# Nine expert blocks chosen early instead of six, and high-word products first

## The chip, the cores and the metric

The kernel runs on one core of one Trainium2 chip. The metric is the device time of one execution in microseconds (us). Three runs of the kernel before gave a median of 1722.14 us (1718.45 to 1723.65).

## The reference

Attention with 32 packed keys per head feeds a dense layer pair, and its 4608 rows `x` of 512 numbers feed a mixture of eight experts:

```python
logits = x @ w_gate                                     # 8 experts
noisy = logits + log1p(exp(x @ w_noise)) * noise
top2 = the two largest of noisy, weights by softmax
for e in range(8): for k in range(2):                   # w1: 512x1024, w2: 1024x512
    out[mask] += weight * (relu(x[mask] @ w1[e]) @ w2[e])
```

Each token goes to two experts, so there are 9216 rows of expert work. Routing the drawn inputs with the reference gives 1138, 1148, 1197, 1127, 1082, 1133, 1212 and 1179 rows for experts 0 to 7. In blocks of 128 rows, the last of each expert padded, that is 75 blocks. Of the first 3456 tokens alone (six of eight batches), the counts are 833, 831, 898, 841, 829, 871, 895 and 914.

## The kernel before, in words

Three phases follow each other. Phase A is the packed attention, phase B the dense layers and the routing of tokens in steps of a batch (`todo`, `at(t, f)`: function f is issued in step t), phase C the expert blocks.

A block is 128 tokens of one expert. Its rows are fetched by four indirect transfers of POOL (`gather`, L978), transposed on DVE and split into a high word `xh` (copied on ACT) and a rest `xl` (subtracted on DVE) (`tx`, L991). `g1` (L1127) multiplies them by the first weights: two halves of 12 matmuls (xh by the high weights, xh by the low, xl by the high), 24 in all, and DVE transposes each half out of PSUM into a tile `h` of which there is one buffer. `tha` (L1149) applies relu in 16 small instructions, shared between ACT and DVE, into a tile `ht` of one buffer, and ACT copies the high word `hh`; `thb` (L1167) subtracts it on DVE to give the rest `hl`. `g2` (L1171) is 24 matmuls with the second weights, ACT scales the result by the gate (y) and POOL adds it to the output by an indirect transfer (store). Weights lie in two slots, each with a first and a second part of 4 MB; SP loads them (`wdma`, L910; `wload`, L1105), and a load is left out when the slot already holds the expert.

To have work while the last tokens are routed, six blocks of one expert with at least 768 rows are chosen from the first six batches (`early_count`, `early_rows`, L884 to L903), in step 214 of phase B. They use slot 0. In `run` (L1198) their PE, SP, DVE and ACT instructions are issued in an order written by hand, and in the same stretch the last tokens are routed (`L.logits`, `route`, `L.rank`, `L.slots`), their places scattered to a table, the remaining blocks planned (`main_rows`, L1003, on DVE), the table read back (`main_table`, `main_tr`), and the gather indices of the main blocks made (`main_sel`, `main_idx`). POOL's transfers wait in a list `queue`; `tick` (L1120) takes one off after each sixth matmul. After the early blocks comes the loop over the main blocks (L1297), in which the order on DVE, ACT and POOL is left to the planner, while PE and SP keep the written order: g1 of block k, then g2 of block k-1. In the early part too, PE runs g1 one block ahead or more: g1(0), g1(1), g2(0), g1(2), g2(1) and so on. The main blocks come alternately from the end of the list of experts and from its start, in slots 1 and 0. With up to 79 blocks in all, 75 are executed always, and those beyond only if they exist (`more`, L1318).

Of the kernel before, what the change touches and what calls it, by code (L numbers as in the profile page):

```python
# [10 lines left out]
F32 = mybir.dt.float32  # L11
FR = mybir.dt.float32r
I32 = mybir.dt.int32
BF = mybir.dt.bfloat16
# [7 lines left out]
P = 128  # L22
# [323 lines left out]
NBLK = 79  # L346
NEARLY = 6
NM = NBLK - NEARLY
# [509 lines left out]
class PhaseC:  # L858
# [16 lines left out]
    def counts(self, name):  # L875
        K, V, mp = self.K, self.K.nc.vector, self.mp
        mb = mp.tile([96, E], BF, name=f"mb{name}")
        V.tensor_copy(mb, K.msum)
        cps = K.pm.tile([P, 512], F32, tag="m", name=f"cps{name}")
        K.nc.tensor.matmul(cps[:, :E], K.ones, mb, start=True, stop=True)  # L880
        return cps


    def early_count(self):  # L884
        K, V, mp = self.K, self.K.nc.vector, self.mp
        self.cps = self.counts("e")

    def early_rows(self):
# [8 lines left out]
        re = mp.tile([NEARLY, 1], F32, name="re")  # L897
        K.nc.gpsimd.iota(re, pattern=[[0, 1]], base=0, channel_multiplier=1, allow_small_or_imprecise_dtypes=True)
        V.scalar_tensor_tensor(re, self.est[:NEARLY], 36.0, re, op0=ALU.mult, op1=ALU.add)
        self.rie = mp.tile([NEARLY, 1], I32, name="rie")  # L900
        V.tensor_copy(self.rie, re)
# [52 lines left out]
    def early_table(self):  # L954
        self.tbe = self.table(self.rie, NEARLY, "e")

    def early_tr(self):
        self.tpse = self.tr(self.tbe, NEARLY, "e")

    def early_tok(self):  # L960
        self.idxe, self.tok4e, self.gatee = self.tok(self.tpse, NEARLY, "e")

    def early_sel(self):
        self.gpse = self.sel(self.tok4e, NEARLY, "e")

    def early_idx(self):
        self.gidxe = self.gidx(self.gpse, NEARLY, "e")


    def slot(self, j):  # L970
        return 0 if j < NEARLY else (j - NEARLY + 1) % 2

    def at(self, j):
        if j < NEARLY:
            return 0, j, self.idxe, self.gidxe, self.gatee
        return self.slot(j), j - NEARLY, self.idx, self.gidxm, self.gate

    def gather(self, k, j=None, pace=None):  # L978
# [5 lines left out]
        rows = (K.x1d[:6 * S] if k < NEARLY else K.x1d).rearrange("n (q y) -> (n q) y", q=4)  # L984
# [18 lines left out]
    def main_rows(self):  # L1003
# [50 lines left out]
        ec, bs, kk = (mp.tile([NM, 1], F32, name=n) for n in ("ec", "bs", "kk"))  # L1054
# [24 lines left out]
    def consts(self):  # L1079
# [21 lines left out]

        self.planr = halves(1, NM, [[1, NM]], 0, "r")
        self.planc = halves(NM, 1, [[0, 1]], 1, "c")

    def wload(self, j, m, hs=(0, 1), after=()):  # L1105
        k = j - NEARLY
# [20 lines left out]
    def g1(self, k, between=None):  # L1127
# [5 lines left out]
        for fc in range(2):  # L1133
            p = self.ph.tile([P, 512], F32, tag="ph", name=f"ph{k}_{fc}")
            n = 0
            for d in range(4):
                for xx, ws in ((xh, 0), (xh, 1), (xl, 0)):
                    self.tick(K.nc.tensor.matmul(p, xx[:, d * P:(d + 1) * P], w[:, fc, ws, d, :], start=(n == 0), stop=(n == 11)))  # L1138
                    n += 1
# [31 lines left out]
    def g2(self, k, between=None):  # L1171
# [6 lines left out]
        for f in range(8):  # L1178
            for xx, ws in ((hh, 0), (hh, 1), (hl, 0)):
                self.tick(K.nc.tensor.matmul(p, xx[:, f * P:(f + 1) * P], w[:, f // 4, ws, f % 4, :], start=(n == 0), stop=(n == 23)))  # L1180
                n += 1
            if f == 3 and between:
                between()
# [14 lines left out]
    def run(self, L):  # L1198
        K, tc = self.K, self.K.tc
        with ExitStack() as ctx:  # L1200
# [15 lines left out]
            M0 = NEARLY  # L1216
# [13 lines left out]

            q += scatters(L.scatter[0]) + gather(4)
# [5 lines left out]
            def half():  # L1237
                route(4)
                self.thb(0)
# [20 lines left out]
            L.store()  # L1260
            self.tha(2, 0)
            rows = self.main_rows()
            next(rows)
            self.g2(1)
# [5 lines left out]
            next(rows, 0)  # L1270
            self.tx(5)
            while q:
                q.pop(0)(self.last)
# [11 lines left out]
            q[:0] = gather(M0 + 1)  # L1285
# [3 lines left out]
            self.g2(4)  # L1289
            self.tx(M0)  # L1290
            self.thb(5)
            while q:
                q.pop(0)(self.last)
# [3 lines left out]
            for k in range(M0, NSURE + 1):  # L1297
# [11 lines left out]
                if k + 1 < NSURE:  # L1309
                    self.wload(k + 1, 1)  # L1310
# [3 lines left out]
            total = K.nc.values_load(self.tmi, min_val=NSURE - 3 - NEARLY, max_val=NM)  # L1314
# [3 lines left out]
    def more(self, j, total):  # L1318
        if j >= NBLK:
            return  # L1320
        with self.K.tc.If(total > j - NEARLY):
# [81 lines left out]
```

## Time and profile before

| what | us |
|---|---|
| three runs | 1722.14 (median), 1718.45, 1723.65 |
| profiled execution, span | 1721.9 |
| PE busy | 1625.7 (94%) |
| DVE, ACT, POOL busy | 1132.5 (66%), 865.1 (50%), 565.5 (33%) |
| first matmul of block 0, g1 of block 9, last result copied | 852.47, 976.33, 1707.97 |

The page gives no other time for the profiled execution than its span. PE holds a matmul for longer than the next one needs to start, so its busy time is read here only for where it is broken. The two levels of its clock are 1.2 and 2.4 GHz; "granted" 1.00 is 2.4 GHz.

### The profile page before, as it was taken

The page shows a single profiled execution, that of the slowest core. Times are in us where ns is not written, and L with a number is a line of the kernel's source. Part 1 is how long each engine was busy: PE and PEld are TensorE (multiplying, and loading weights), DVE is VectorE, ACT ScalarE, POOL GpSimd, SP SyncE. Part 2 cuts the span into 40 slices and gives each one's busy share as a digit, 9 for nine tenths or more (in the row PEclk, how much of TensorE's full clock was granted, in tenths as well). Part 3 has the DMA queues.
Part 4 walks back from the last instruction along what each step waited for, and adds up shares of the span by engine and source line. Part 5 has one row for each costly group of instructions (what it writes and reads, how often), then busy time and mean ns, then how long its engine had stood idle before and what let it go on. Part 6 is the DMA issues. An engine that isn't in the chain of part 4 may idle for free.

```text
span 1721.9 us, 29366 instructions
## 1 busy us (share of the span) xinstructions
PE 1625.7 (94%) x10031; PEld 1378.8 (80%) x10031; DVE 1132.5 (66%) x2903; ACT 865.1 (50%) x1824; POOL 565.5 (33%) x559
## 2 busy tenths in 40 slices
PE   5667999999999999999997999999999999999996
PEld 3334889898989898989976788888888888888885
DVE  7886867676767676866573566666666666666652
ACT  3444555555555555543365455555555555555552
POOL 0000200021212121242543754544555454444421
PEclk7677999999999999999998999999999999999998
DMA  8784267686878787752366572255622457227541
GB/s 275 230 272 130 83 208 250 203 245 203 232 240 243 235 248 232 252 174 55 95 174 231 158 242 51 49 145 185 209 47 47 141 156 240 48 48 239 156 124 26
DMA packets 145653, 293.59 MB, mean 171 GB/s; under 512 B 19682, under 2 KB 69130, under 8 KB 140380
## 3 DMA queue, kind: packets, MB, share of 16 engines
q1 hardware_dynamic: 121676, 252.17, 44.1%
q0 software_dynamic: 23824, 39.51, 12.7%
q8 instruction: 80, 1.31, 0.3%
q14 instruction: 73, 0.60, 0.1%
HBM read 695.73 MB, written 107.59 MB: 467 GB/s over the span
## 4 chain that ended last, share of the span: by engine, by line
PE 86%; DVE 7%; DMA 3%; issue 1%; ACT 1%; POOL 1%; POOLq 0%; DVEq 0%; ACTq 0%
PE ph L1138 23%; PE py L1180 22%; PE acc L501 22%; PE h L476 12%; PE u L442 2%; PE s L175 2%; DMA out_dram<-y,idxe 1%; PE tp L199 1%; PE pv L211 1%; PE sq L299 1%; PE lg L522 1%; DMA kT<-in_kT_dram 1%; DVE nm L180 1%; DVE cva L76 1%; POOL x L986 0%
## 5 line engine op out<-in xcount | busy, mean ns | idle before, releaser
L1160 ACT ACTIVATE ht<-h 32x256 f32<-32x256 f32 x636 | 264.7, 416 | 239.8 <-DVE h L1140 224.7
L1138 PE MATMUL ph<-w0s,xh 128*128 128x512 f32 x1200 | 376.6, 395 | 3.2 <-ACT xh L97 2.9
L1180 PE MATMUL py<-w1s,hh 128*128 128x512 f32 x1200 | 375.8, 395 | 2.6 <-ACT hh L1164 2.6
L986 POOL DMA_INDIRECT x<-x1d,gidxm x276 | 266.2, 964 | 317.2 <-DVE xt L996 224.2
L501 PE MATMUL acc<-gh,wol 128*128 128x288 f32 x1024 | 302.2, 295 | 0.3 <-POOL wol L101 0.3
L501 PE MATMUL acc<-gh,woh 128*128 128x288 f32 x1024 | 301.6, 295 | 0.0
L501 PE MATMUL acc<-gl,woh 128*128 128x288 f32 x1024 | 301.3, 294 | 0.0
L1140 DVE STREAM_TRANSPOSE h<-ph 128x512 f32<-128x512 f32 x150 | 107.4, 716 | 267.7 <-PE ph L1138 267.5
L1138 PEld LDWEIGHTS ph<-w0s,xh 128*128 128x128 f32 x1200 | 226.3, 189 | 54.9 <-ACT xh L97 3.3
L1180 PEld LDWEIGHTS py<-w1s,hh 128*128 128x128 f32 x1200 | 228.1, 190 | 52.2 <-ACT hh L1164 3.2
L1180 PE MATMUL py<-w1s,hl 128*128 128x512 f32 x600 | 236.4, 394 | 2.3 <-DVE hl L1169 2.3
L1138 PE MATMUL ph<-w0s,xl 128*128 128x512 f32 x600 | 236.8, 395 | 0.0
L657 POOL DMA_INDIRECT table<-d,qi x96 | 96.5, 1006 | 307.1 <-DVE g L485 208.5
L501 PEld LDWEIGHTS acc<-gh,wol 128*128 128x128 f32 x1024 | 192.6, 188 | 0.5 <-POOL wol L101 0.5
L501 PEld LDWEIGHTS acc<-gh,woh 128*128 128x128 f32 x1024 | 193.0, 188 | 0.0
L501 PEld LDWEIGHTS acc<-gl,woh 128*128 128x128 f32 x1024 | 192.7, 188 | 0.0
L1158 DVE TENSOR_SCALAR ht<-h 32x256 f32<-32x256 f32 x564 | 173.4, 307 | 10.3
L483 ACT ACTIVATE t<-h 128x288 f32<-128x288 f32 x256 | 104.3, 407 | 148.3 <-PE h L476 147.7
L476 PE MATMUL h<-a2h,uh 128*128 128x288 f32 x512 | 159.6, 312 | 2.7 <-DVE g L485 1.8
L97 ACT ACTIVATE gh<-g 128x288 fp32r<-128x288 f32 x256 | 113.2, 442 | 86.9 <-DVE g L485 86.0
L485 DVE TENSOR_TENSOR g<-h,t 128x288 f32<-128x288 f32 x256 | 115.7, 452 | 57.8 <-ACT t L483 57.1
L476 PE MATMUL h<-a2h,ul 128*128 128x288 f32 x512 | 151.6, 296 | 0.2 <-DVE ul L451 0.2
(235 smaller groups left out, 2387.3 us busy)
## 6 DMA issues: line engine op xcount, KB each, us to landing
w0s<-wsp SPq DMA_DIRECT2D x142, 2048.0 KB
w1s<-wsp SPq DMA_DIRECT2D x142, 2048.0 KB
wsp<-wt SPq DMA_DIRECT2D x128, 512.0 KB
wt<-in_w_dram SPq DMA_DIRECT2D x128, 256.0 KB
kT<-in_kT_dram SPq DMA_DIRECT2D x16, 608.0 KB
out_dram<-zero SPq DMA_DIRECT2D x37, 256.0 KB
v<-in_v_dram SPq DMA_DIRECT2D x16, 576.0 KB
q<-in_qT_dram SPq DMA_DIRECT2D x32, 288.0 KB
```

The source lines that it names most:

```text
L97: nc.scalar.activation(hi, src, AF.Copy)
L476: nc.tensor.matmul(h[:, :TN], u[:, G, fs], x[:, G, :], start=(n == 0), stop=(n == 5))
L483: nc.scalar.activation(t, h[:, :TN], AF.Tanh)
L485: PACE[0] = nc.vector.tensor_tensor(g, h[:, :TN], t, op=ALU.subtract).ins
L501: nc.tensor.matmul(ACC[ch][d][:, :TN], w[:, d * P:(d + 1) * P], x, start=(f == 0 and n == 0), stop=(f == 15 and n == 2))
L657: ins = nc.gpsimd.indirect_dma_start(out=K.table, out_offset=IO(ap=qi[:, i:i + 1], axis=0), in_=d[:, i, :], in_offset=None, oob_is_err=True)
L986: g = K.nc.gpsimd.indirect_dma_start(out=x[:, b, :], out_offset=None, in_=rows, in_offset=IO(ap=gidx[:, c, b:b + 1], axis=0))
L1138: self.tick(K.nc.tensor.matmul(p, xx[:, d * P:(d + 1) * P], w[:, fc, ws, d, :], start=(n == 0), stop=(n == 11)))
L1140: self.last = V.transpose(h[:, 2 * fc:2 * fc + 2].rearrange("p g n -> p (g n)"), p).ins
L1158: V.tensor_scalar(dst, src, 0.0, None, op0=ALU.max)
L1160: K.nc.scalar.activation(dst, src, AF.Relu)
L1180: self.tick(K.nc.tensor.matmul(p, xx[:, f * P:(f + 1) * P], w[:, f // 4, ws, f % 4, :], start=(n == 0), stop=(n == 23)))
```

## The change

Besides the six early blocks of one expert, up to three early blocks of the last expert are taken (`NTOP`), as far as full blocks of its rows exist; a block that does not exist gets gate zero. They use slot 1, whose second weights for the last expert are now loaded right after the last rows are stored, without the wait for the table's transfer. The order written by hand covers nine blocks; table, indices and first main weights move to later places. In both products all high-word matmuls come first, the eight or four with the low word last. The loop runs over 66 main blocks instead of 69.

```diff
-NBLK = 79
 NEARLY = 6
-NM = NBLK - NEARLY
+NTOP = 3
+NE = NEARLY + NTOP
+NM = 79 - NEARLY
+NBLK = NE + NM
 def early_rows(self):
+        top = mp.tile([P, 1], F32, name="top")
+        V.tensor_scalar(top, self.est, float(E - 1), -128.0 * NEARLY, op0=ALU.is_equal, op1=ALU.mult)
+        V.tensor_tensor(top, top, self.cps[:, E - 1:E], op=ALU.add)
+        V.tensor_scalar(self.valid, K.need, top, None, op0=ALU.is_le)
+        V.tensor_reduce(self.ntop, self.valid[:, NEARLY:], axis=AX.X, op=ALU.add)
...
+        V.scalar_tensor_tensor(self.ke, K.last, self.ntop, self.ke, op0=ALU.mult, op1=ALU.add)
 def early_tok(self):
+        self.K.nc.vector.tensor_tensor(self.gatee, self.gatee, self.valid, op=ALU.mult)
 def slot(self, j):
-        return 0 if j < NEARLY else (j - NEARLY + 1) % 2
+        return 0 if j < NEARLY else 1 if j < NE else (j - NE + 1) % 2
 def main_rows(self):
+        V.tensor_scalar(k7, ec, float(E - 1), self.ntop[:NM], op0=ALU.is_equal, op1=ALU.mult)
+        V.tensor_tensor(ec, ec, k7, op=ALU.add)
 def consts(self):
+        V.tensor_scalar(K.need, K.need, 128.0, None, op0=ALU.mult)
+        V.memset(K.need[:, :NEARLY], -1e6)
+        V.tensor_scalar(K.last, K.eio, float(E - 1), None, op0=ALU.is_equal)
+        V.tensor_scalar(K.needc, K.early[:, 0:1], 128.0, 128.0 * (1 - NEARLY), op0=ALU.mult, op1=ALU.add)
+        V.tensor_scalar(K.early[:, 1:2], K.early[:, 0:1], 36.0 * (E - 1) - NEARLY, None, op0=ALU.add)
+        V.tensor_scalar(K.early[:, 2:3], K.early[:, 0:1], float(NEARLY), None, op0=ALU.is_ge)
+        V.scalar_tensor_tensor(K.early[:, 0:1], K.early[:, 2:3], float(-NEARLY), K.early[:, 0:1], op0=ALU.mult, op1=ALU.add)
 def g1(self, k, between=None):
-            for d in range(4):
-                for xx, ws in ((xh, 0), (xh, 1), (xl, 0)):
+            for xx, d, ws in [(xh, d, ws) for d in range(4) for ws in range(2)] + [(xl, d, 0) for d in range(4)]:
 def g2(self, k, between=None):
-        for f in range(8):
-            for xx, ws in ((hh, 0), (hh, 1), (hl, 0)):
+        for xx, f, ws in [(hh, f, ws) for f in range(8) for ws in range(2)] + [(hl, f, 0) for f in range(8)]:
 def run(self, L):
             def half():
+                self.thb(0)
                 route(4)
-                self.thb(0)
...
+            mb = self.sums("m")
             self.tx(3)
-            def half():
-                L.rank()
-                self.cps = self.counts("m")
-                self.thb(1)
-                L.slots()
-            self.g1(2, half)
+            self.g1(2, lambda: self.thb(1))
+            L.rank()
+            self.cps = self.counts("m", mb)
+            L.slots()
...
             L.store()
+            for h in range(2):
+                self.wdma(1, 1, h, E - 1)
...
             self.main_table()
-            for h in range(2):
-                self.dep(self.wdma(1, 1, h, E - 1), self.tbg, "the small transfer goes first")
-            self.wload(M0, 0)
-            self.wload(M0, 1)
+            q += gather(7)
             self.g1(4, lambda: self.thb(3))
             self.tha(4, 0)
-            self.main_tr()
-            self.g2(3, self.main_sel)
-            self.main_idx()
-            self.gather(M0)
+            self.g2(3)
+            self.tx(6)
+            q += gather(8)
             self.g1(5, lambda: self.thb(4))
             self.wload(M0 + 1, 0)
             self.tha(5, 0)
             self.g2(4)
+            self.main_tr()
+            self.tx(7)
+            def half():
+                self.main_sel()
+                self.thb(5)
+            self.g1(6, half)
+            self.main_idx()
+            q += gather(M0)
+            self.tha(6, 0)
+            self.g2(5)
+            self.wload(M0 + 1, 1)
+            self.tx(8)
+            q += gather(M0 + 1)
+            self.g1(7, lambda: self.thb(6))
+            self.tha(7, 0)
+            self.g2(6)
+            self.g1(8, lambda: self.thb(7))
+            self.wload(M0, 0)
             self.tx(M0)
+            self.tha(8, 0)
+            self.g2(7)
+            self.thb(8)
```

## Rows read from the trace of the kernel before

**Rows 1.** Stages view: us, then busy us (count) by engine, clock, DMA share, GB/s

```profile
852.47:976.33 123.86, 107.21 (x439) 84.78 (x438) 66.51 (x209) 64.78 (x137) 63.47 (x62) 0.90 0.65 210
```

**Rows 2.** Waits of PE from 848 to 985: total, times, longest us

```profile
PE tpsm L930 <- DMA tbm<-table,ri: 6.8, 1, 6.8
PE ph L1138 <- ACT xh L97: 2.9, 1, 2.9
PE py L1180 <- ACT hh L1164: 2.6, 1, 2.6
PE py L1180 <- DVE hl L1169: 2.3, 1, 2.3
PE cpsm L880 <- DVE mbm L878: 1.7, 1, 1.7
```

**Rows 3.** Timeline of PE at three gaps: start us, us, what, idle before

```profile
867.74 0.50 PE L1180 MATMUL py<-w1s,hl 128*128 128x512 f32 x1 [2.28 <-DVE hl L1169]
...
871.72 0.62 PE L1180 MATMUL py<-w1s,hh 128*128 128x512 f32 x2
...
879.27 0.71 PE L1138 MATMUL ph<-w0s,xh 128*128 128x512 f32 x2
...
933.87 1.22 PE L1138 MATMUL ph<-w0s,xh 128*128 128x512 f32 x2 [2.88 <-ACT xh L97]
...
940.16 0.63 PE L1138 MATMUL ph<-w0s,xh 128*128 128x512 f32 x2
```

**Rows 4.** Chain of waits, two of its pieces: start us, us, what

```profile
987.43 5.60 PE ph L1138 x24
...
1691.42 5.60 PE ph L1138 x24
```

**Rows 5.** Timeline of ACT in the early blocks

```profile
863.61 1.06 ACT L1164 ACTIVATE hh<-ht 128x1024 fp32r<-128x1024 f32 x1
...
880.61 6.81 ACT L1160 ACTIVATE ht<-h 32x256 f32<-32x256 f32 x16
...
892.42 6.82 ACT L1160 ACTIVATE ht<-h 32x256 f32<-32x256 f32 x16 [2.81 <-DVE hl L1169]
...
904.12 6.79 ACT L1160 ACTIVATE ht<-h 32x256 f32<-32x256 f32 x16 [2.55 <-DVE hl L1169]
```

**Rows 6.** Timeline of DVE in the early blocks

```profile
864.34 0.17 DVE L567 TENSOR_SCALAR den<-u 96x24 f32<-96x24 f32 x1
...
866.47 1.22 DVE L1169 TENSOR_TENSOR hl<-ht,hh 128x1024 fp32r<-128x1024 f32 x1
...
876.23 0.89 DVE L996 STREAM_TRANSPOSE xt<-x 128x128 f32<-128x128 f32 x4
...
902.84 1.18 DVE L1169 TENSOR_TENSOR hl<-ht,hh 128x1024 fp32r<-128x1024 f32 x1
```

**Rows 7.** Timeline of DVE: first and last of 18 constants; after step 214

```profile
283.78 0.14 DVE L1090 CAST hir<-halfr 1x73 int32<-1x73 f32 x1
...
286.70 0.15 DVE L1099 TENSOR_SCALAR evenc<-oddc 73x1 f32<-73x1 f32 x1
...
743.12 0.82 DVE L101 TENSOR_TENSOR wt<-wt 128x512 fp32r<-128x512 f32 x1 [2.68 <-ACT wt L97]
```

**Rows 8.** Timeline of PE behind those constants

```profile
287.66 0.41 PE L476 MATMUL h<-a2h,uh 128*128 128x288 f32 x1
```

**Rows 9.** Timeline of POOL: the table's transfer, a store that waited

```profile
903.05 2.73 POOL L918 DMA_INDIRECT tbm<-table,ri  x1 [0.30 <-issue]
...
941.85 1.57 POOL L1188 DMA_INDIRECT out_dram<-y,idxe  x1 [11.71 <-DMA out_dram<-y,idxe]
```

**Rows 10.** Timeline of DVE at the start of the loop

```profile
960.34 0.89 DVE L996 STREAM_TRANSPOSE xt<-x 128x128 f32<-128x128 f32 x4 [2.34 <-DMA x<-x1d,gidxm]
961.15 0.67 DVE L1140 STREAM_TRANSPOSE h<-ph 128x512 f32<-128x512 f32 x1
```

**Rows 11.** Transfers by line, whole span: count, median us from issue to landing

```profile
x<-x1d,gidxm POOLq DMA_INDIRECT x276, 2.6
```

More of the change, by code (lines that the diff above doesn't have):

```diff
@@ L873, in dep, with sums, counts @@
         self.K.tc.add_manual_dep(ins.ins, i.name, mybir.DependencyInfo(mybir.DependencyClass.Sync, mybir.DependencyReason.DATA), reason=reason)
[L875 to L878, printed above, removed]
+    def sums(self, name):
+        mb = self.mp.tile([96, E], BF, name=f"mb{name}")
+        self.K.nc.vector.tensor_copy(mb, self.K.msum)
+        return mb
+    def counts(self, name, mb):
+        K = self.K
         cps = K.pm.tile([P, 512], F32, tag="m", name=f"cps{name}")
@@ L983, in gather @@
         x = self.X[k]
-        rows = (K.x1d[:6 * S] if k < NEARLY else K.x1d).rearrange("n (q y) -> (n q) y", q=4)
+        rows = (K.x1d[:6 * S] if k < NE else K.x1d).rearrange("n (q y) -> (n q) y", q=4)
         for b in range(4) if j is None else (j,):
@@ L1053, in main_rows @@
         V.tensor_tensor(l2, cum[:NM], cc.to_broadcast([NM, E]), op=ALU.is_le)
-        ec, bs, kk = (mp.tile([NM, 1], F32, name=n) for n in ("ec", "bs", "kk"))
+        ec, bs, kk, k7 = (mp.tile([NM, 1], F32, name=n) for n in ("ec", "bs", "kk", "k7"))
         V.tensor_reduce(ec, l2, axis=AX.X, op=ALU.add)
@@ L1177, in g2 @@
         n = 0
-        for f in range(8):
-            for xx, ws in ((hh, 0), (hh, 1), (hl, 0)):
-                self.tick(K.nc.tensor.matmul(p, xx[:, f * P:(f + 1) * P], w[:, f // 4, ws, f % 4, :], start=(n == 0), stop=(n == 23)))
-                n += 1
-            if f == 3 and between:
+        for xx, f, ws in [(hh, f, ws) for f in range(8) for ws in range(2)] + [(hl, f, 0) for f in range(8)]:
+            self.tick(K.nc.tensor.matmul(p, xx[:, f * P:(f + 1) * P], w[:, f // 4, ws, f % 4, :], start=(n == 0), stop=(n == 23)))
+            n += 1
+            if n == 12 and between:
                 between()
@@ L1214, in run @@
                 self.wdma(1, 0, h, E - 1)
-            M0 = NEARLY
+            M0 = NE
             q = self.queue
@@ L1229, in scatters, with flush @@
                 return [lambda i, j=j: s(j, i) for j in range(6)]
+            def flush(n):
+                while len(q) > n:
+                    q.pop(0)(self.last)
             q += scatters(L.scatter[0]) + gather(4)
@@ L1263, in run @@
             next(rows)
+            q += gather(6)
             self.g2(1)
@@ L1270, in run @@
             next(rows, 0)
+            flush(4)
             self.tx(5)
-            while q:
-                q.pop(0)(self.last)
             self.main_table()
-            for h in range(2):
-                self.dep(self.wdma(1, 1, h, E - 1), self.tbg, "the small transfer goes first")
-            self.wload(M0, 0)
-            self.wload(M0, 1)
+            q += gather(7)
             self.g1(4, lambda: self.thb(3))
             self.tha(4, 0)
-            self.main_tr()
-            self.g2(3, self.main_sel)
-            self.main_idx()
-            self.gather(M0)
-            q[:0] = gather(M0 + 1)
+            self.g2(3)
+            flush(4)
+            self.tx(6)
+            q += gather(8)
             self.g1(5, lambda: self.thb(4))
@@ L1289, in run @@
             self.g2(4)
+            flush(4)
+            self.main_tr()
[5 more added lines that the diff above has]
+            self.main_idx()
+            flush(0)
+            q += gather(M0)
[7 more added lines that the diff above has]
+            self.g2(6)
+            flush(4)
+            self.g1(8, lambda: self.thb(7))
+            self.wload(M0, 0)
             self.tx(M0)
-            self.thb(5)
-            while q:
-                q.pop(0)(self.last)
+            self.tha(8, 0)
+            self.g2(7)
+            self.thb(8)
+            flush(0)
             self.count = None
@@ L1320, in more @@
             return
-        with self.K.tc.If(total > j - NEARLY):
+        with self.K.tc.If(total > j - NE):
             ks = range(j, min(j + 2, NBLK))
```

51 lines of the change are left out of this document (32 added, 19 removed).

## The prediction

> **What bounds the kernel now.** I read the page's busy shares, then the stages view, PE's waits, the timelines of PE, ACT, DVE and POOL around its gaps, and the chain of waits. PE is the bound nearly everywhere. In the loop nothing stops it: two pieces of the chain 64 blocks apart start 703.99 us apart, 11.00 us a block or 0.229 a matmul [rows 4]. The weak stretch lies between the first matmul of block 0 (852.47) and g1 of block 9 (976.33). PE passes 408 matmuls there (eight blocks and one g1), 93.5 us at the loop's pace, and some 2.3 us of routing and index products; it takes 123.86, of which it is idle 16.65 [rows 1]. About 28 us are lost. Five waits make up 16.3 of it [rows 2]: the first rest hl (2.3), the count (1.7), the table (6.8), the first main block's xh (2.9), hh of block 7 (2.6). The remainder is the clock: the stretch has a granted mean of 0.90 [rows 1]. After the gap of 2.28 us the matmuls ran at 1.2 GHz until about 871.7, after the one of 2.88 until about 940; after the one of 1.71 (879.27) they were at 2.4 GHz at once [rows 3]. The half rate lasted 4.0 and 6.3 us, so such a gap costs 2.0 to 3.1 us more than itself.
>
> **The change, step by step.** First what it adds ahead of the blocks. The constants get seven more small DVE instructions. Today's 18 run from 283.78 to 286.85, 0.17 us each [rows 7], and the h product behind them starts at 287.66, just when DVE has read its PSUM tile, its first matmul drawn out to 0.41 us [rows 8]: there is no slack. 7 x 0.17 = **1.2 us** late; bounds 0 (the planner of todo puts nothing else there, but DVE may catch up) and 1.4 (seven at 0.2). Step 214 gets eleven more, 1.5 to 2.2 us; right behind it DVE idles 2.68 us waiting for ACT [rows 7], which hides them; without that cover it would be 2 us. The extra gate product and index columns in steps 234 to 237 are one instruction of 0.15 us: nothing.
>
> Then the blocks; times are on today's axis, the 1.2 us added at the end. The new order lets g2(0) begin with 16 high-word matmuls, 3.7 us, so it needs hh(0) at 864.67 [rows 5], and hl(0) only at 868.5. Today hl(0) is queued on DVE behind routing and starts at 866.47; moved ahead of it, it starts at 864.7, and routing ends 0.3 us later than today [rows 6]. The 2.3 us gap and its slow matmuls go. One risk: matmul 9 of g2(0) needs the second half of the weights loaded at 852.8, which may still be arriving at 866.6; today that half is first used after 871. I take 0, the bound is 2 us and 2 for the clock.
>
> What is late next is ACT. In every early block from 2 on, all 16 relus are on it, in a ring through single buffers: relus 6.8, hh 1.06, y(k-1) and xh(k+2) on ACT, then xl, one transpose of h and hl on DVE, and only then may the next relus write ht. Today relus(2) start 880.61, relus(3) 892.42, relus(4) 904.12, each released by hl [rows 5]: **11.70 us a block, against PE's 11.00**. Today PE is late enough not to feel it; with its gaps gone it will run into it. In the new order relus(2) start at 876.23 + 0.3 + 0.15 (the earlier count cast) + 4.4 as today [rows 6] + 0.6 for a transpose that now stands ahead = 881.6. Relus(3) come 11.65 later, 893.3, then every 11.7: 905.0, 916.7, 928.4, 940.1. Each g2(k) can start when hh(k) is there, 7.9 us after its relus: 889.5, 901.2, 912.9, 924.6, 936.3, 948.0 for k = 2 to 7. Its 16 high words last about as long as hl(k) is behind hh(k) (904.02 against 900.33 for block 3, 3.7 us [rows 5, 6]), so hl no longer stops PE. In front of relus(8) stands x of the first main block: hl(7) 1.2, transposes 1.6, xh 0.6, so 951.4, hh(8) at 959.3. g2(8) ends at **964.8**, where g1 of block 10 starts; today that is 987.43 [rows 4]. On the way PE waits about 0.9 (rank), 1.4 (g2(2)), and 0.1 to 0.7 six times, 4.9 us in all, no gap above 1.4.
>
> The other moved steps are covered. The table's gather goes out when the plan is ready, 900 as today plus 0.3 for two added instructions, and lands 7.8 us later [rows 2, 9] at 908.5; main_tr now stands behind g2(4), 918.4. The second weights of slot 1 are moved on SP ahead of it, and the six scatters then share the engines with 4 MB. A store under such a load held POOL 11.7 us [rows 9]; with as much on the last scatter (issued by 891) the table lands by 911, and with the same again on its own gather 915 to 918, still not late; beyond that PE waits one for one. Gathers of blocks 6 to 8 and of the two first main blocks are issued five us or more ahead of their transposes even with that landing time. SP's loads for block 10 start at 912 and 931, needed at 965 and 976. Three early blocks only change places with main ones: 75 blocks before and after.
>
> The loop's start keeps one hazard. Today the planner put the transposes of x two and three blocks ahead in front of block 7's first h transpose, so this one ran at 961.15, behind a gather landing [rows 10], and hh(7) was 2.6 late. The same order would now put block 10's behind block 12's gather: block 11's gathers are held until g1(9) is transposed, 963, eight issues of 1.25 end at 973, landing 2.6 later [rows 11] at 975.8, hh(10) 7.2 on (as today from 960.34 [rows 10] to the end of hh(7) at 967.5) at 983.0, while g2(10) wants it at 981.4. I take **1.6 us**; bounds 0 (other order) and 2.6 + 3.1 as today.
>
> Sum: 987.4 - (964.8 + 1.2 + 1.6) = 19.8 us off the span of 1721.9, which is 0.2 us from the runs' median; the last blocks and the tail are the same instructions. **1702.4 us**. The reordered matmuls keep their number, shapes and weight loads, so I cost their pace at nothing; a pace different by 0.1% would be 1 us.
>
> **Rivals.** (1) Cleaner: chain and hazard are milder, PE's own order decides. Without any gap, g1(10) starts 28 us earlier less 1.2: 1695; between that and my case lies 1695 to 1699. For it: all DMA is hidden. Against: the 11.70 ring is measured. (2) The loop's hazard or the late weights make a gap above 2 us: a slow stretch follows, 4 to 9 us more than my case's, 1705 to 1711. For it: my stall of 1.6 lies just under the 1.71 that cost no clock. (3) The small gaps in each round drop the clock again and again. Today's rows show it after 2.28 and 2.88 us and not after 1.71, and my gaps are shorter. Each drop costs 2.0 to 3.1; a slow round takes 13.5 us, has no gap, and so one round in two would fall: four to six drops, 8 to 16 us, 1710 to 1718. The Trainium skill ("TensorE: Matmul & The Clock Gate", "A second HAM failure mode: psum-queue depth-cycling") says that frequent short pauses between groups of matmuls can make the clock oscillate; by it the time would be that of this case, and today's 1.71 us gap speaks against it. (4) Slower: the three blocks of the last expert do not exist at step 214. This decides at fewer than 384 counted rows (1152 if that expert is also the first choice). Then slots of early work are empty, the main blocks exceed 66, and the conditional tail runs one or two pairs of blocks without overlap: at least 22 us a pair, and with gathers, weights and relus in line up to 45, minus my gain: 1724 to 1790. Against: the reference's routing has 914 rows of the last expert in the first six batches and 833 of expert 0, which is then the first choice. A table landing after 944 instead of 911 would end on the same side. (5) The order of high words or the plan buys nothing because PE is held elsewhere by the same amount: 1717 to 1727.
>
> **How the numbers follow.** My case (1699 to 1705) 50%, (1) 15%, (2) 18%, (3) 8%, (4) 4%, (5) 5%. The runs cannot tell a change under about 0.3%, 5 us, from none. Faster by more: my case, (1), (2) and most of (3), 0.89; same 0.06; slower 0.05. Eight times in ten: 1696 to 1711; that leaves out the tail of (1), (3), (4) and (5).
>
> **What would show it.** The table wait and the first hl wait gone from PE's waits; relus of blocks 2 to 7 every 11.7 us, each released by hl, and PE's gaps ahead of g2 released by hh; a new wait of 1.2 us of an h product near 288; g1(10) near 966; the loop at 11.00. Wrong if the loop runs at another pace, if gaps above 2 us or a granted clock well under 1 appear between 860 and 965, or if conditional blocks run behind block 74.

## The result, and the profile after

The changed kernel takes **1701.46 us** (median of 4 runs, 1699.79 to 1702.16), the kernel before 1720.68 beside it (4 runs, 1718.45 to 1723.65): ratio 0.9888, 95% interval 0.9876 to 0.9901. The prediction was 1702.4. Later the changed kernel ran again, on another chip: 1698.66 against 1722.26, ratio 0.9861 (0.9845 to 0.9877); the profiled execution of that run was disturbed and is not used.

The profile after is of an execution of 1702.0 us with a span of 1700.3, so 1.7 us lie around a span. By the same 1.7 the span of 1721.9 before belongs to the run of 1723.65, not to the median. Span against span the change took 21.6 us off, median against median 19.2.

The first thing to read is the weak stretch, first matmul of block 0 to the start of g1(10). View: stages (us, then busy us and count of PE, PEld, DVE, ACT, POOL, granted clock, DMA share, GB/s).

```profile
853.11:965.43 112.32, 109.02 (x488) 87.02 (x487) 61.88 (x193) 78.18 (x171) 59.02 (x54) 1.00 0.74 230
```

PE is idle 3.30 us in it and the clock is 1.00 throughout; before, 16.65 us and 0.90 [rows 1]. The waits of PE in 848 to 985 (total, times, longest) are down to two of any size:

```profile
PE py L1214 <- ACT hh L1199: 1.8, 4, 0.8
PE py L1214 <- DMA w1s<-wsp: 1.5, 1, 1.5
```

The table, xh and first hl, which led that list before [rows 2], are gone. PE's own timeline of the stretch (start, us, instruction, idle before it) shows where the two stand:

```profile
868.96 2.11 PE L1214 MATMUL py<-w1s,hh 128*128 128x512 f32 x8 [1.49 <-DMA w1s<-wsp]
...
890.41 3.93 PE L1214 MATMUL py<-w1s,hh 128*128 128x512 f32 x16 [0.82 <-ACT hh L1199]
...
901.97 3.93 PE L1214 MATMUL py<-w1s,hh 128*128 128x512 f32 x16 [0.32 <-ACT hh L1199]
...
919.15 0.35 PE L949 MATMUL tpsm<-ident,tbm 73*128 73x73 f32 x2
...
959.85 3.93 PE L1214 MATMUL py<-w1s,hh 128*128 128x512 f32 x16 [0.31 <-ACT hh L1199]
...
965.43 2.01 PE L1173 MATMUL ph<-w0s,xh 128*128 128x512 f32 x8
```

The wait of 1.49 is for the second half of block 0's second weights; the 8 matmuls behind it take 2.11 us, full rate. tpsm has no wait at all. g1(10) starts at 965.43; before, 987.43 [rows 4]. The view of transfers gives 7.3 us from issue to landing for the table; issued at 905.08 it landed at 912.4, 6.8 us before tpsm. ACT's timeline shows what paces the blocks between:

```profile
882.47 6.80 ACT L1195 ACTIVATE ht<-h 32x256 f32<-32x256 f32 x16
...
894.00 6.82 ACT L1195 ACTIVATE ht<-h 32x256 f32<-32x256 f32 x16 [2.55 <-DVE hl L1204]
...
940.25 6.82 ACT L1195 ACTIVATE ht<-h 32x256 f32<-32x256 f32 x16 [2.55 <-DVE hl L1204]
...
951.38 6.80 ACT L1195 ACTIVATE ht<-h 32x256 f32<-32x256 f32 x16
```

From 894.00 to 940.25 the relus of blocks 3 to 7 begin every 11.56 us, each released by hl: ACT's ring, as [rows 5] had it at 11.70. The loop's start shows on DVE, and the loop's pace in the chain of waits (start, us, what):

```profile
975.12 0.89 DVE L1016 STREAM_TRANSPOSE xt<-x 128x128 f32<-128x128 f32 x4 [2.73 <-DMA x<-x1d,gidxm]
975.93 0.67 DVE L1175 STREAM_TRANSPOSE h<-ph 128x512 f32<-128x512 f32 x1
```

```profile
981.14 1.07 ACT hh L1199
...
982.25 5.73 PE py L1214 x24
987.99 5.48 PE ph L1173 x24
...
1669.99 5.48 PE ph L1173 x24
```

Block 10's h transpose stands behind x of block 12, as foreseen from [rows 10]. From 987.99 to 1669.99 are 62 blocks of 11.00 us, as in [rows 4]: the loop is untouched, and all of the gain lies ahead of it.

### The profile page after: what moved, and what is told of

It is laid out like the page before. It is cut to its first block, busy times and chain, and to the rows that moved or that the text cites. A ratio compares the mean times of both kernels' runs of the same rounds, so it can differ in the third digit from the quotient of the medians.

```text
span 1700.3 us, 29332 instructions
## 1 busy us (share of the span) xinstructions
PE 1617.0 (95%) x10031; PEld 1372.1 (81%) x10031; DVE 1127.2 (66%) x2900; ACT 873.9 (51%) x1848; POOL 569.9 (34%) x560
## 4 chain that ended last, share of the span: by engine, by line
PE 84%; DVE 7%; ACT 4%; DMA 2%; issue 1%; POOL 1%; POOLq 0%; DVEq 0%; ACTq 0%
PE acc L503 23%; PE py L1214 21%; PE ph L1173 21%; PE h L478 12%; ACT ht L1195 2%; PE u L444 2%; PE s L175 1%; PE tp L199 1%; PE pv L211 1%; PE sq L299 1%; PE lg L524 1%; DVE cva L76 0%; DMA kT<-in_kT_dram 0%; DVE hl L1204 0%; DMA cvr<-in_w_out_dram 0%
## 5 line engine op out<-in xcount | busy, mean ns | idle before, releaser
L1195 ACT ACTIVATE ht<-h 32x256 f32<-32x256 f32 x660 | 274.7, 416 | 229.8 <-DVE h L1175 209.9
L1006 POOL DMA_INDIRECT x<-x1d,gidxm x264 | 254.9, 966 | 277.1 <-DVE xt L1016 203.2
L1173 PE MATMUL ph<-w0s,xh 128*128 128x512 f32 x1200 | 301.8, 393 | 0.0
L1214 PE MATMUL py<-w1s,hh 128*128 128x512 f32 x1200 | 286.8, 391 | 3.4 <-ACT hh L1199 1.8
L1214 PEld LDWEIGHTS py<-w1s,hh 128*128 128x128 f32 x1200 | 224.6, 188 | 54.6 <-ACT hh L1199 4.7
L1193 DVE TENSOR_SCALAR ht<-h 32x256 f32<-32x256 f32 x540 | 166.5, 308 | 9.9
L1173 PE MATMUL ph<-w0s,xl 128*128 128x512 f32 x600 | 162.6, 393 | 0.0
L487 DVE TENSOR_TENSOR g<-h,t 128x288 f32<-128x288 f32 x256 | 115.7, 452 | 57.0 <-ACT t L485 56.5
L478 PE MATMUL h<-a2l,uh 128*128 128x288 f32 x512 | 151.4, 296 | 0.0
```

Of the source, the lines that this page charges most:

```text
L478: nc.tensor.matmul(h[:, :TN], u[:, G, fs], x[:, G, :], start=(n == 0), stop=(n == 5))
L487: PACE[0] = nc.vector.tensor_tensor(g, h[:, :TN], t, op=ALU.subtract).ins
L1006: g = K.nc.gpsimd.indirect_dma_start(out=x[:, b, :], out_offset=None, in_=rows, in_offset=IO(ap=gidx[:, c, b:b + 1], axis=0))
L1193: V.tensor_scalar(dst, src, 0.0, None, op0=ALU.max)
L1195: K.nc.scalar.activation(dst, src, AF.Relu)
```

## The experiments

Two measures serve besides the time, since the start of block 0 differs from execution to execution for reasons ahead of it (848.8 to 853.1 in the traces of the first comparison, e1 to e4, e10 and e11, 854.0 to 857.5 in those of e5 to e8 and e12), and since the kernels ran in five batches, each on one chip beside its own runs of the kernel before: the first comparison, e1 to e4, e5 to e8, e9 to e11, and e12. Both are read from PE's timelines: from the first matmul of g1(0) to that of g1(2), which holds the wait for w1s, and from there to g1(10), eight blocks. "w1s" is the wait for its second half.

| kernel | w1s | g1(0) to g1(2) | to g1(10) | sum | ratio to before |
|---|---|---|---|---|---|
| before | none | 22.0 | 113.0 | 135.0 | 1 |
| after | 1.5 | 19.6 | 92.7 | 112.3 | 0.9888, 0.9861 |
| e2 nine, old order | 2.8 | 21.8 | 99.9 | 121.7 | 0.9921 |
| e3 relus shared | 5.4 | 26.0 | 99.9 | 125.9 | 0.9937 |
| e4 constants spread | 2.9 | 21.0 | 92.5 | 113.5 | one run |
| e5 shared, pinned | 5.6 | 26.8 | 90.5 | 117.2 | 0.9949 |
| e6 three edits | 5.9 | 25.9 | 89.4 | 115.3 | 0.9921 |
| e7 load behind table | 5.2 | 26.1 | 89.6 | 115.7 | 0.9923 |
| e8 table wanted early | 6.7 | 27.4 | 101.8 | 129.2 | 0.9999 |
| e10 load held | 3.6 | 24.6 | 89.6 | 114.2 | 0.9878 |
| e11 all mended | 3.9 | 23.6 | 89.4 | 113.0 | 0.9880 |
| e12 scatters later | 1.7 | 20.4 | 100.3 | 120.7 | 0.9945 |

In the batch of e5 to e8 and in that of e12 the kernel before took 1736.9 and 1736.3 us (see the last section), so their ratios are compared with each other only.

**e1: the order alone.** The kernel before with the new order of the products, and hl(0) ahead of routing.

```diff
-        for f in range(8):
-            for xx, ws in ((hh, 0), (hh, 1), (hl, 0)):
+        for xx, f, ws in [(hh, f, ws) for f in range(8) for ws in range(2)] + [(hl, f, 0) for f in range(8)]:
...
-                route(4)
                 self.thb(0)
+                route(4)
```

> The kernel before with the high words first in both products and hl(0) ahead of the routing instructions on DVE; still six early blocks. Theory (the gaps do not add up: the table's landing is set by DVE and POOL, so a PE that is earlier only waits longer there): the 2.3 us wait on hl goes, the table's wait grows from 6.8 to 9 to 11 us, the time changes by 0 to -2 us, about 1719.5. Rival (each gap is worth its length and its slow stretch): -4 to -5 us, about 1716.

Measured: 1722.99 against 1720.71, ratio 1.0013 (1.0003 to 1.0024). Waits of PE in 848 to 985:

```profile
PE tpsm L930 <- DMA tbm<-table,ri: 7.2, 1, 7.2
PE cpsm L880 <- DVE mbm L878: 3.0, 1, 3.0
...
PE py L1178 <- DMA w1s<-wsp: 2.0, 1, 2.0
PE rk L619 <- DVE Mb L607: 0.8, 1, 0.8
```

The hl wait of 2.3 [rows 2] is gone, and its time is in the next things PE meets: w1s (2.0, not waited for before), rank (0.8), and the count (3.0 after 1.7). The count's gap of 1.71 us cost no clock before [rows 3]; behind the one of 2.98 the 8 matmuls take 3.76 us, half rate. The table's wait, which the theory saw growing to 9 to 11 us, is 7.2, and the time rose by 2.3 instead of falling by 0 to 2: the theory was right that the gaps do not add up as savings, and missed where the time would go. The order of the products alone is worth nothing here.

**e2: the blocks alone.** The changed kernel with the old order in both products.

```diff
-        for xx, f, ws in [(hh, f, ws) for f in range(8) for ws in range(2)] + [(hl, f, 0) for f in range(8)]:
+        for f in range(8):
+            for xx, ws in ((hh, 0), (hh, 1), (hl, 0)):
```

> The changed kernel with the old order of matmuls (high, low, rest in triples) in both products. Theory (the ring through ACT's relus sets the pace of blocks 2 to 8, so PE falls behind once by the 3 us that hl is behind hh, pays one slow stretch and then keeps pace): 4 to 7 us slower than the changed kernel, 1705.5 to 1708.5, one gap of about 3 us on hl, later ones under 1 us. Rival (every g2 of the early blocks stops 3 us for hl): 15 us or more slower, over 1716. Rival (only the first wait of the kernel before comes back): +2 to +4.

Measured: 1707.38, ratio 0.9921 (0.9908 to 0.9934), 5.9 us above the changed kernel. Its largest wait on PE, and what DVE did ahead of it:

```profile
929.44 0.79 PE L1216 MATMUL py<-w1s,hl 128*128 128x512 f32 x1 [3.55 <-DVE hl L1205]
```

```profile
925.37 0.89 DVE L1016 STREAM_TRANSPOSE xt<-x 128x128 f32<-128x128 f32 x4 [5.93 <-DMA x<-x1d,gidxe]
926.96 0.69 DVE L101 TENSOR_TENSOR xl<-xt,xh 128x512 fp32r<-128x512 f32 x1 [0.70 <-ACT xh L97]
927.57 0.71 DVE L1176 STREAM_TRANSPOSE h<-ph 128x512 f32<-128x512 f32 x1
928.20 1.18 DVE L1205 TENSOR_TENSOR hl<-ht,hh 128x1024 fp32r<-128x1024 f32 x1
```

hl(5) stood on DVE behind a transpose that waited 5.93 us for a gather. In the old order the third matmul of g2 needs hl; in the new one the seventeenth does, 3.7 us on. So the nine blocks are worth about 13 us (1720.71 - 1707.38), and the order 6 us on top of them, of which it gave nothing by itself. The 6 us are in the main this one gap and the half rate behind it; a gather that was late made it, so how much of them another execution would lose is not shown.

**e3: the ring taken away.** Every early block from 2 on gets four of its 16 relus on DVE.

```diff
-            self.tha(2, 0)
+            self.tha(2, 1)
...
             next(rows)
-            self.tha(3, 0)
             self.g2(2)
...
-            self.tha(8, 0)
+            self.tha(8, 1)
```

Blocks 3 to 7 are edited as 2 and 8, and block 3's call goes ahead of the `next(rows)`.

> The changed kernel with 4 of the 16 relus of blocks 2 to 8 on DVE (and block 3's ahead of the second part of the plan). Theory (the relus on ACT are the bound of the early blocks): ACT's ring falls from 11.56 to about 9.9 us, under PE's 11.0, the waits on hh (0.8 and four of 0.3 us) go, 2 us faster, about 1699.4. Rival (DVE, in order, becomes the bound, or PE is held elsewhere): no change or slower, 1701 to 1705, with the gaps on DVE.

Measured: 1711.11, ratio 0.9937 (0.9923 to 0.9952), 9.6 us above the changed kernel: as a forecast of the time the theory fell. POOL and PE:

```profile
913.11 1.60 POOL L1222 DMA_INDIRECT out_dram<-y,idxe  x1 [10.66 <-DVE xt L1016]
...
917.92 1.88 POOL L937 DMA_INDIRECT tbm<-table,ri  x1 [0.30 <-issue]
```

```profile
931.33 0.49 PE L949 MATMUL tpsm<-ident,tbm 73*128 73x73 f32 x2 [8.29 <-DMA tbm<-table,ri]
```

The planner, which orders POOL, had put the store of y(2) ahead of the table's transfer; in the changed kernel that starts at 905.08. The store did not wait for y(2), which ACT had ready at 904.1: the chain of waits shows the store of y(1), issued at 900.83, taking 11.40 us, and each store goes only when the one before it has landed, like the one that waited 11.71 [rows 9]. The releaser that the line names, xt, had nothing to do with it. The table, whose rows were known at 905.67, stood behind the store and a gather, and PE waited 8.29 us for it. ACT's ring did become faster, as the theory had it: the relus of blocks 4 and 5 begin 9.85 us apart.

**e4: the constants spread.** The seven new constants one in each of the steps 60 to 66, where DVE has other work of the same kind.

```diff
+        for i in range(7):
+            at(60 + i, C.const, i)
```

> The changed kernel with its seven new constant instructions issued one each in steps 60 to 66 instead of all in step 44. Theory (they stop PE there): PE's wait of an h product on DVE's g, 2.4 us in three waits, goes back to the 1.8 us in two of the kernel before, and block 0 starts 0.6 us earlier, at 852.5. Rival (they cost nothing there, the 0.6 us is from elsewhere): block 0 stays at 853.1.

Measured: 1700.61, one run. The wait of PE for g at the h product, over 100 to 1700, in the changed kernel and then in e4:

```profile
PE h L478 <- DVE g L487: 2.4, 3, 1.1
```

```profile
PE h L478 <- DVE g L487: 1.8, 2, 1.1
```

So the constants cost 0.6 us, not 1.2: half of them was absorbed. The time of one run cannot show 0.6. Block 0 started at 850.42, which fits neither side: its start differs by more than 0.6 between executions anyway.

**e5: e3 with POOL's order pinned.** One line more than e3: the store of y(2) depends on the table's transfer.

```diff
+            if k == 2:
+                self.dep(g, self.tbg, "behind the table")
```

> The kernel after with every early block's relus shared with DVE, as in e3, and one more rule: the store of y(2) goes behind the table's transfer on GpSimd, as it does in the kernel after. Theory (e3's +9.6 us came from that one exchange on GpSimd's queue, whose store waited for y(2) and held the table's transfer to 917.9): the transfer is issued at 905 to 907 again, the wait at tpsm falls from 8.3 us to under 1, the waits for hh stay away, and the time is 1699 to 1703 plus what the second half of w1s is late (1.5 to 5.4 us so far). Rival (the shared relus themselves cost it, by making DVE late with ri and the order of the chain): ri at 905.5 and a transfer at 907 or later still leave over 4 us at tpsm, and the time stays at 1707 or above.

Measured: 1727.23 against 1736.91, ratio 0.9949 (0.9933 to 0.9964). POOL, and PE's waits in 848 to 985:

```profile
911.86 1.85 POOL L937 DMA_INDIRECT tbm<-table,ri  x1 [3.04 <-issue]
...
919.77 1.63 POOL L1222 DMA_INDIRECT out_dram<-y,idxe  x1 [3.51 <-ACT hh L1199]
```

```profile
PE py L1214 <- DMA w1s<-wsp: 5.6, 1, 5.6
PE py L1214 <- DVE hl L1204: 0.7, 1, 0.7
```

The wait at tpsm is gone by the order alone, and the eight blocks take 90.5 us instead of 99.9: the exchange on POOL's queue cost e3 its 9 us. The time did not come to the expected size; the 5.6 us for w1s are in it.

**e6: three small edits together.** Constants as in e4; relus shared in blocks 4 to 8 only, which leaves POOL's order as it was; g2(0) takes the first half of its weights with high and low words before the second half.

```diff
-            self.tha(4, 0)
+            self.tha(4, 1)
...
+        if k == 0:
+            order = order[:8] + order[16:20] + order[8:16] + order[20:]
```

> The kernel after with three edits: the seven constants one in a step each (as in e4); relus shared with DVE in blocks 4 to 8 alone, which leaves GpSimd's and SyncE's orders as they are; and in g2(0) alone the first half of the weights with high and low words before the second half, so that the second half of w1s is wanted 0.9 us later. Theory: waits at h back to 1.8 in 2 (gain 0.6), waits for hh only in g2(2) and g2(3) (gain 0.6), the wait for w1s 0.9 shorter than it would have been: 0 to 2 us less than the kernel after, 1699 to 1702, which the timing can hardly tell from it, so the trace's waits decide. Rival (DVE gets late by the added relus): a wait for h or xl of more than 1 us in blocks 4 to 10, and a time above 1703.

Measured: 1722.41, ratio 0.9921 (0.99 to 0.9942), the batch of e5. The wait for w1s was 5.9 us all the same, and no other wait of PE between 862 and 975 reached 0.3 us. Eight blocks take 89.4 us, PE's own pace. The rival (DVE late) is out; the time stays unclear, as there is no run of the changed kernel in that batch.

**e7: the w1s load of the last expert behind the table.**

```diff
-            for h in range(2):
-                self.wdma(1, 1, h, E - 1)
...
             self.main_table()
+            for h in range(2):
+                self.dep(self.wdma(1, 1, h, E - 1), self.tbg, "the small transfer goes first")
```

> The kernel after with the two loads of the last expert's second product (w1s) put behind the table's transfer, where the kernel before has them, not ahead of it. Theory: the table's transfer starts by up to 4 us earlier (901 to 905), because nothing of the load is in the scatters' way any more; TensorE does not notice, since the table is not wanted before 919; the weights start at about 908 and are wanted at 936.9, so the time is 1700 to 1703, as the kernel after. Rival (three late transfers of 4 MB each push each other past their use): a wait of 2 to 6 us for w0s or w1s at g2(6), g1(9) or g2(8), and 1704 to 1708.

Measured: 1723.70, ratio 0.9923 (0.9896 to 0.9949), as e6. The table's transfer:

```profile
912.53 2.44 POOL L937 DMA_INDIRECT tbm<-table,ri  x1 [2.65 <-DMA out_dram<-y,idxe]
```

That is 29.0 us after g1(2) began; with the load ahead it was 32.4 (after), 29.4 (e5), 30.3 (e8) and 28.9 (e10). So the moved load does not hold the table up by more than other executions differ, and PE does not notice either way. No late weights: the rival is out too. The move of that load, a step of the change, is worth nothing that shows.

**e8: one and a half blocks of cover taken away.** The table's transposes ahead of g2(3) and not ahead of g1(6).

```diff
+            self.main_tr()
             self.g2(3)
...
-            self.main_tr()
             self.tx(7)
```

> The kernel after with the transposes of the table ahead of g2(3), where they come at 902, and not ahead of g1(6) at 919: one and a half blocks of cover taken away. Theory (the three new blocks pay by standing between the table's transfer and its first reader): TensorE stands until the table has landed, 908.5 to 918 by the transfers seen, so a wait of 7 to 15 us at tpsm, up to 2 us of slow products behind it, less 0.6 to 1 us since the relus catch up meanwhile: 1707 to 1717. Rival (the table is there when wanted and the gain comes from the order of the products): a wait under 3 us and a time below 1704.

Measured: 1736.46, ratio 0.9999 (0.9985 to 1.0014), so 13 us above e6 and e7 of the same batch (0.0077 of 1736.9), and no gain at all over the kernel before.

```profile
919.10 0.49 PE L949 MATMUL tpsm<-ident,tbm 73*128 73x73 f32 x2 [9.65 <-DMA tbm<-table,ri]
919.33 6.38 PE L1214 MATMUL py<-w1s,hh 128*128 128x512 f32 x16
```

The wait is 9.65 us, and the 16 matmuls behind it take 6.38 instead of 3.93, at a granted clock of 0.50 from 915 to 920 and 0.54 from 920 to 925. Wait and slow matmuls are 12.1 us, and the sum in the table is 13.5 to 13.9 above those of e7 and e6. This is the experiment that carries the explanation. The added blocks pay because they stand between the table's transfer and its first reader.

**e9: the changed kernel again**, unedited, in the batch of e10 and e11.

> The kernel after, unchanged, on the chip of the two runs that follow it, so that these are compared with it and not only with the kernel before. Expected: the ratio of the first comparison, 0.987 to 0.990 to the kernel before; on a chip where the second half of w1s lands as late as in e5 to e8 (waits of 5.2 to 6.7 us, against 1.5 in the kernel after before), 0.990 to 0.993.

Measured: 1698.66 against 1722.26, ratio 0.9861 (0.9845 to 0.9877), a little below what was expected.

**e10: the next load held back.** The load of w0s for the last expert, issued right behind w1s, waits for block 1's second h transpose.

```diff
-            for h in range(2):
-                self.wdma(1, 0, h, E - 1)
...
             self.g1(1, half)
+            for h in range(2):
+                self.dep(self.wdma(1, 0, h, E - 1), self.last, "the load wanted first goes alone")
```

> The kernel after with one edit: the load of w0s for the last expert, issued right behind that of w1s at 854.5, waits until block 1's second h transpose (about 864), so that w1s is loaded alone. Theory (the second half of w1s is late in g2(0) because the next load runs beside it): the wait for w1s in g2(0) is under 0.5 us, and the kernel is 1.0 to 1.5 us below the kernel after on a chip where that wait was 1.5 us, 4 to 6 below it on one where it was 5 to 6. The held load lands by 880 and is wanted at 919. Rival (the small transfers on GpSimd's queue, scatters and gathers, hold the load up): the wait stays within 1 us of that of the kernel after, and so does the time.

Measured: 1700.96, ratio 0.9878 (0.9862 to 0.9895). PE, and the stage in which it waits (the last number is GB/s):

```profile
866.79 3.78 PE L1214 MATMUL py<-w1s,hh 128*128 128x512 f32 x8 [3.61 <-DMA w1s<-wsp]
```

```profile
860.00:865.00 5.00, 3.18 (x14) 2.18 (x12) 4.31 (x13) 1.02 (x1) 3.43 (x3) 1.00 0.88 216
865.00:870.00 5.00, 3.21 (x8) 2.54 (x9) 3.93 (x17) 3.93 (x10) 0.86 (x1) 0.60 0.90 183
```

The held load was issued at 865.17, 16.0 us after that of w1s and 1.6 before the wait ended, and the wait was longer, 3.6 us: the theory fell, and the wait that the rival foresaw, within 1 us of 1.5, was passed as well. The engines moved 216 and 183 GB/s at 88% and 90% busy. The time is neither better nor worse than that of e9 beside it: the intervals of the two ratios overlap.

**e11: held load, spread constants, relus shared in blocks 4 to 8.** The edits of e10, e4 and the first of e6's diff.

> The held load of e10, the constants one in a step each as in e4, and relus shared with DVE in blocks 4 to 8 alone, which leaves GpSimd's order as it is. Theory: the gains of the parts are waits of TensorE at different places and add: 0.6 (constants), 0.6 (hh in blocks 4 to 8) and what the held load gives, so 2 to 3 us below the kernel after where that load's wait was 1.5 us, 5 to 7 below it where it was 5 to 6. Rival (the time goes to the next wait, as it did in e1): the sum is not more than e10's.

Measured: 1701.50, ratio 0.9880 (0.9863 to 0.9897). The only wait of PE that the view lists for 848 to 985:

```profile
PE py L1219 <- DMA w1s<-wsp: 3.9, 1, 3.9
```

The sum is 1.2 below that of e10 and above that of the changed kernel, and the time is no better than either's: the rival holds. The table shows why. In e6, e7, e10 and e11 the wait for w1s is 3.6 us or more, and then the eight blocks behind it take 89.4 to 89.6 us, whether relus are shared (e6, e11) or not (e7, e10); with the short wait of the changed kernel they take 92.7. While PE waits for weights, ACT's ring gets ahead by as much, and PE meets no hh wait afterwards. The late load and the ring hide each other: mending one shows the other. That both together would give about 3 us (92.7 - 89.4), and the wait besides, is an estimate: no version has both mended. None of these versions beats the changed kernel.

**e12: the scatters out of the load's way.** The first six scatters come behind g2(0).

```diff
-            q += scatters(L.scatter[0]) + gather(4)
+            q += gather(4)
...
             self.g2(0)
+            q[:0] = scatters(L.scatter[0])
...
-            q[:0] = scatters(L.scatter[1])
+            q += scatters(L.scatter[1])
```

> The kernel after with one edit: the first six scatters into the table, on GpSimd's queue from 857 to 865 and so beside the load of w1s, come behind g2(0), ahead of the other six; the gathers of x for blocks 4 and 5 go in their place. Theory (the scatters hold up the load: in every kernel the rate falls from about 400 to 180 to 320 GB/s between 860 and 870, and holding back the next load did not help): the wait for w1s in g2(0) falls below 1 us, the lowest so far being 1.5, and the time is 0.5 to 4 us below the kernel after by how late w1s was. The second six scatters end 2 to 4 us later and the table's transfer with them, at 905 to 909; it is wanted at 919. Rival (any transfers of GpSimd's hold it up, or the load is late by itself): the wait stays at 1.5 to 6 us and the time within 0.3% of the kernel after, or above it if the table is now waited for.

Measured: 1726.61 against 1736.30, ratio 0.9945 (0.9929 to 0.9962). Stages, and PE's first two waits on transfers:

```profile
865.00:870.00 5.00, 5.00 (x24) 4.02 (x23) 3.37 (x8) 3.32 (x7) 0.00 (x0) 1.00 1.02 419
870.00:875.00 5.00, 3.29 (x15) 2.42 (x14) 3.92 (x17) 1.70 (x4) 0.94 (x1) 1.00 1.04 436
```

```profile
PE tpsm L949 <- DMA tbm<-table,ri: 6.9, 1, 6.9
...
PE py L1214 <- DMA w1s<-wsp: 1.7, 1, 1.7
```

With the scatters later the engines move 419 to 436 GB/s; POOL issued no transfer at all from 863.9 to 873.9. The issue of the load on SP (start, us, engine, transfer, count), here and in the changed kernel:

```profile
858.78 0.92 SPq L931 DMA_DIRECT2D w1s<-wsp  x2
```

```profile
853.49 0.92 SPq L931 DMA_DIRECT2D w1s<-wsp  x2
```

From there to the first matmul on the second half are 13.5 us in e12 (872.27) and 15.5 in the changed kernel (868.96); in the other ten kernels, e1 to e8, e10 and e11, it was 16.0 to 19.4. So the load was 2 us faster, in one execution. It does not show that the scatters hold the load up, since the changed kernel's own trace speaks against it:

```profile
856.00:858.00 2.00, 2.00 (x15) 1.32 (x15) 1.18 (x2) 0.00 (x0) 0.93 (x1) 1.00 1.04 442
858.00:860.00 2.00, 2.00 (x14) 1.68 (x14) 0.36 (x1) 0.00 (x0) 1.03 (x2) 1.00 1.01 426
860.00:862.00 2.00, 2.00 (x10) 1.66 (x10) 1.88 (x8) 1.28 (x4) 0.99 (x2) 1.00 0.98 410
862.00:864.00 2.00, 2.00 (x10) 1.65 (x10) 1.08 (x4) 1.94 (x6) 1.56 (x2) 1.00 1.11 205
```

Five scatters are issued between 854.95 and 861.80, and up to 862 the engines move as much as without them. The rate falls in the stretch in which the sixth is issued, here and in e10 (164 GB/s from 858 to 860), and stays low in e10 after it; whether the scatters do that, or the gathers, or the end of the load itself, stays open.

The wait did not fall below 1 us, and the theory fell in favour of the rival. In part this is because in its batch the load is issued 3.1 us after block 0 has started, not 0.4 as in the changed kernel's profile: e5 to e8 had 2.9 to 3.2, which explains a good part of their longer waits. And PE waited 6.9 us for the table: it was issued 36.2 us after g1(2) began, 3.8 later than in the changed kernel, and took 17.1 from issue to reader. The loss is larger than the gain.

## Why the prediction was right

The forecast rested on one thing: that the early blocks fill the time in which the table travels, so that its wait and those behind it go, with ACT's ring as the next limit. g1(0) to g1(10) was to take 964.8 - 852.47 = 112.3 us, and it took 112.3. e8 shows the mechanism by taking the cover away: 13 us, all of the gain that its batch showed. e1 and e2 show that the order of the products gives nothing without the blocks, and 6 us with them in the one execution of e2 that was profiled, which the prediction's sum did not separate. That 112.3 met 112.3 to the tenth is in part luck, as the steps show.

By its steps:
- **Constants**: 1.2 forecast, 0.6 measured (e4), inside the bounds 0 to 1.4.
- **hl(0) gap**: gone. The risk behind it, the second half of w1s, was taken at 0 with a bound of 2 + 2; the wait is 1.5 us without loss of clock, and in the other versions 1.7 to 6.7, beyond that bound. It cost the end little because the ring then had slack (e10, e11). That is a compensation the prediction did not have.
- **ACT's ring**: 11.70 a block forecast, 11.56 measured. Counted from block 0's start, relus(2) begin at 29.4 (forecast 881.6 - 852.47 = 29.1) and relus(8) at 98.3 (98.9). Five rounds of the ring took 0.7 us less than forecast, and 0.3 was lost ahead of them; from relus(8) to g1(10) it took 14.0 us instead of 13.4, since xh of the first main block came ahead of hh(8). PE's gaps were to sum to 4.9 us; it is idle 3.3, and differently: none for rank, 0.82 instead of 1.4 at g2(2), three of 0.3 instead of six of 0.1 to 0.7, and the 1.5 for w1s that stood at 0.
- **The table**: forecast to land at 908.5 to 918, wanted at 918.4. It landed at 912.4 and was wanted at 919.15, with 6.8 us to spare. It went out at 905.08 and not at 900.3. The plan was ready at 901.0, and what POOL stood for in the 4.6 us ahead of the transfer the trace does not name; before, too, it started at 903.05 [rows 9], later than the 900 that the prediction took. Its 7.3 us from issue to landing is near the 7.8 that was used. From issue to reader it was 7.1 where the reader waited for it in e8, 13.4 in e3, 17.1 in e12; with the last it would have landed at 922.2, 3 us late. "Covered" was right in this execution, and is not sure for every one.
- **Loop start**: 1.6 forecast, under 0.3 measured: g2(10) starts at 982.25, 0.13 us behind PE's work ahead of it and right behind the end of hh(10), 129.1 us after block 0 (982.21 - 853.11) and not 130.5 (983.0 - 852.47). The order of DVE was the one foreseen, and from x's transpose to the end of hh it took 7.1 us, as forecast (7.2). What was sized wrong is the landing of x: its transpose began 122.0 us after block 0 and not 123.3. The 2.6 us of [rows 11] run from the start of an issue (972.53 to 975.12 here), and the prediction added them to the end of the last one.
- **Sum**: 19.8 off the span; 21.6 measured. Constants and loop start account for 0.6 + 1.3 = 1.9 of the difference. The saving was thus forecast 1.8 too small; on the other side the prediction took the span of 1721.9 for the time of a run near the median, and a run takes 1.7 more than its span. These two cancel for the profiled execution, 1702.0 against 1702.4; the median, 1701.46, lies another 0.5 lower. That the forecast came within 1 us is in part luck.

Of the rivals, (2) and (3) needed a gap over 2 us or repeated drops of the clock: the longest gap was 1.49 and the clock 1.00. By the rule of the Trainium skill that (3) named ("TensorE: Matmul & The Clock Gate", "A second HAM failure mode: psum-queue depth-cycling") short frequent pauses could have made the clock oscillate; four pauses of 0.31 to 0.82 us ahead of g2 did not. (1) failed on the ring, (4) and (5) on the result itself.

## What to carry to other kernels

A wait for a long transfer is best removed by putting independent work between the transfer and its reader, and the profile tells in advance how much work fits and which engine paces it. Before mending the next wait, ask which slack it feeds: a late load and a slow ring can hide each other, and then mending either gives nothing. In a queue that a planner orders, a change elsewhere can exchange two entries, and a store that waits, here for the one before it to land (e3), then holds every transfer behind it; compare the order of each queue before and after, and pin what matters.

## What was not expected of the hardware

**The clock after a gap.** A gap of 2.88 us halved the clock for what followed in the kernel before [rows 3]. A gap of 2.88 in e4 did not: 8 matmuls took 2.14 us.

```profile
867.66 2.14 PE L1219 MATMUL py<-w1s,hh 128*128 128x512 f32 x8 [2.88 <-DMA w1s<-wsp]
```

Behind 3.61 (e10) the same 8 took 3.78, and behind 2.98 in e1 3.76. So the length of a gap alone did not decide between 2.28 and 2.88 us; what does was not tried.

**A busy share without a rate.** Towards the end of the 4 MB load e10 moved 216 and 183 GB/s at a DMA share of 0.88 to 0.90; e12 moved 419 to 436 at 1.02 to 1.04, and the changed kernel 442 at 1.04 and, 6 us later, 205 at 1.11. A high share is no sign of a high rate. Which transfers kept the engines busy in the slow stretches was not found.

**A stretch without instructions.** In the batch of e5 to e8 and in that of e12, every profiled kernel ran short of instructions at block 11's first product, g1(11), here in e6: PE's timeline and a stage.

```profile
987.90 0.58 PE L1178 MATMUL ph<-w0s,xl 128*128 128x512 f32 x1 [1.55 <-issue]
990.00 0.59 PE L1178 MATMUL ph<-w0s,xl 128*128 128x512 f32 x1 [1.51 <-issue]
```

```profile
990.00:995.00 5.00, 1.76 (x3) 0.58 (x2) 0.00 (x0) 0.00 (x0) 3.78 (x5) 0.50 0.19 54
```

PE waits for no semaphore, DVE and ACT run dry behind it, and some 20 us pass. The kernel before was 16 us longer in the same two batches than in the others; that the same stretch is in it was not seen, since no trace of it was taken there. Why it appears in some batches stays open.
